# Handing Wo over from layer A to layer B: tiles cut to A's ending tiles, an earlier norm for B's second group, and a second bf16 row tile

## The chip, the cores and the metric

One core of a Trainium2 chip runs the whole kernel as one program. The metric is the device time of one execution in microseconds (us); the time of the kernel before is the median of 7 runs. The profile is one further execution with the hardware profiler on, whose span (first to last instruction) and own time are given below.

## The reference, cut to what matters

Activations x are [2048, 640]. Four layers follow one another, A, B, A, B, each adding its result to x after a layer norm without scale or offset:

```python
x = A_x
x = x + _A_ref(_layernorm(x), A_wq, A_wk, A_wv, A_wo, A_beta)
x = x + _B_ref(_layernorm(x), B_mem0, B_Wq, B_Wk, B_Wv, B_Wo, 32)
x = x + _A_ref(_layernorm(x), ...)      # same weights
x = x + _B_ref(_layernorm(x), ...)      # same weights
```

Layer A is causal attention of 32 heads of 20 in four blocks of 512 tokens, with a running memory `M`, `z` mixed in by a gate, and ends with `o @ wo`. Layer B is a recurrence over 64 segments of 32 tokens:

```python
for s in range(64):
    h = concat([mem, x[32*s:32*s+32]])          # 8 + 32 rows
    q, k, v = h @ Wq, h @ Wk, h @ Wv            # 32 heads of 128
    p = softmax(mask(q @ k.T * scale))
    o = einsum('bhte,hed->btd', p @ v, Wo)      # Wo: 32 heads x 128 x 640
    mem, out = o[:8], o[8:]                     # mem feeds the next segment
```

So every segment of B needs all 32 heads of `Wo` before it can hand its memory to the next one. `Wo` is 5.2 MB in bf16, and it is loaded anew for each of the two B layers.

## The kernel before, in words

**Order of the work.** All compute engines but SP (TensorE = PE, VectorE = DVE, ScalarE = ACT, GpSimd = POOL) run in the order in which the program writes the instructions: the wrapper `_OrdEng` ties each instruction to the one before it on its engine, which is why nearly all rows of the profile have its line, L87. The DMAs issued from SP are not tied in this way; a scheduler places them, and SP then issues them strictly one after another, each after its own waits. A DMA also waits for an earlier DMA on the same of eight completion lanes. Buffers come from pools; a tile may start to be written when the last reader of what lay there before is done.

**The end of layer A.** A's last eight half-row products, `outp(3, 0..7)` (tiles `a_YP`, one pair per row tile `tt` of 128 rows), are kept back as `br.tail` and are run among the first projections of B. Each pair adds the residual rows, giving the fp32 row tile (`a_xo` in the first handover, `a_xr` itself in the second), stores it to `xres` (L518), has POOL cast it to the bf16 tile `a_xb` (one buffer), and stores that to `xres_bf` (L521). The tiles of A that live until then are, on the right side of SBUF, `a_oT` (5120 bytes in each partition), `a_wvo` (6400) and `a_xb` (1280) in the pool `a_out`, and `a_xr`, `a_xo` in `a_out2`; and on the left side the pool `a_tail`, which `tail_tiles` fills with two residual rows and, in the first handover, an output row.

**Wo.** One head of `Wo` is 1280 bytes in each partition. Heads 0 to 10 (`EARLY`, `NEARLY` = 11) are loaded during the last block of A into tiles of A that are free by then (`a_wo`). Head 11 goes into a pool of its own (`b_wo1`), loaded from ACT's queue among B's first projections. Heads 12 to 15 (`b_wo3`, where `a_tail` was) and 16 to 31 (`b_wo2`, one tile of 16 heads in two loads, where A's `a_out` and `a_out2` were) are issued from SP once `a_tail` and `outer` are closed (L942 and L944). All of the second tile is taken to depend on all that lay under it.

**The start of layer B.** First come six tail units (`b_tail`: Q, K and V of the 32 last-rows of group 0; a group is 4 segments, 128 rows), then four first projections (`b_first`), each after one pair of A's tail. Then the loop over segments: `b_Qa`, `b_Ka`, `b_Qb`, `b_Kb` (projections; DVE turns each through one of two `b_TQ` buffers, DVE and POOL place it), `b_SP` (scores, three PSUM buffers shared with the projections), `b_V`, `b_OTL` (values) and `b_OPS`, the product with `Wo`: a first half with heads 0 to 15, and a second half in pairs (16,20) (17,21) (18,22) (19,23) (24,28) (25,29) (26,30) (27,31). The memory rows of `b_OPS` go through `b_TM` on DVE into `b_hT`, for which the next segment's `b_Qa` waits.

**The norm of group 1.** `ln_dma(1)` loads its rows at B's start. In segment 0 `ln_norm(1)` runs after the first values (two `BATCH_NORM_STATS2`, an aggregate, an add on DVE, a power on POOL), `ln_apply(1)` writes `b_xn` on DVE, and `ln_tr(1)` issues a transposing DMA to `b_xnTg` (L738), followed by the load of group 2's rows (L723). `tail_cols(1)` then copies columns of it to `b_hx` on POOL at the start of the tail units of segment 1; for later groups it runs in the segment before.

Of the kernel before, what the change touches and what calls it, by code (L numbers as in the profile page):

```python
# [19 lines left out]
BF16 = mybir.dt.bfloat16  # L20
# [3 lines left out]
PSUM = bass.MemoryType.PSUM  # L24

S_TOK = 2048
NW1 = 12
EARLY = [(tag, h0, n, at) for tag, h0, n in (("a_phiks", 0, 1), ("a_MZ32", 1, 2), ("a_xnT0", 3, 4), ("a_vaug0", 7, 4)) for at in range(n)]
NEARLY = len(EARLY)
ORDER_ENGINES = ("tensor", "scalar", "vector", "gpsimd")  # L30
D = 640
# [23 lines left out]
def layernorm_stats(nc, pool, C, xt, name):  # L55
    stats = pool.tile([128, 2, nc.vector.BN_STATS_DIM], F32, name=f"{name}_st", tag="ln_st")
    nc.vector.bn_stats(out=stats[:, 0, :], in_=xt[:, 0:320])
    nc.vector.bn_stats(out=stats[:, 1, :], in_=xt[:, 320:640])
    mv = pool.tile([128, nc.vector.BN_AGGR_DIM], F32, name=f"{name}_mv", tag="ln_mv")
    nc.vector.bn_aggr(out=mv[:], in_=stats[:])  # L60
    rstd = pool.tile([128, 1], F32, name=f"{name}_rstd", tag="ln_rstd")
    nc.vector.tensor_scalar(out=rstd[:], in0=mv[:, 1:2], scalar1=LN_EPS, scalar2=None, op0=ALU.add)
    nc.gpsimd.tensor_tensor(out=rstd[:], in0=rstd[:], in1=C.mhalf[:, 0:1], op=ALU.pow)
    return mv, rstd


def layernorm_apply(nc, xt, xn_out, mv, rstd):
    nc.vector.tensor_scalar(out=xn_out.rearrange("p (g jj d) -> p jj g d", jj=2, d=32),
                            in0=xt.rearrange("p (jj g d) -> p jj g d", jj=2, d=32),
                            scalar1=mv[:, 0:1], scalar2=rstd[:, 0:1], op0=ALU.subtract, op1=ALU.mult)  # L70
# [130 lines left out]
def layer_A(nc, nc_raw, tc, C, W, A_wv, A_wo, x_src, x_dst, xb_dst, src_is_bf16, general, outer, mem0, wo_src, prep=None, prefetch=()):  # L201
# [5 lines left out]
    with ExitStack() as ctx:  # L207
        br = Bridge()
        bp = outer.bridge.enter_context(tc.tile_pool(name="a_bridge", bufs=1, side="right", reuse_waits="tile"))
        so = outer.enter_context(tc.tile_pool(name="a_out", bufs=1, side="right", reuse_waits="tile"))  # L210
# [116 lines left out]
        def run(gctx):  # L327
# [13 lines left out]
            us, xin = {}, {}  # L341
# [158 lines left out]
            def res_load(n, tt):  # L500
                r0 = n * 512 + tt * 128
                xr = so2.tile([128, D], xdt, name="a_xr")
                nc_raw.sync.dma_start(xr[:], x_src[r0:r0 + 128, :])
                xin[tt] = xr

            def outp(n, i):
                tt, half = divmod(i, 2)
                if half == 0 and (tt, "o") not in xin:
                    xin[tt, "o"] = so2.tile([128, D], F32, name="a_xo") if src_is_bf16 else xin[tt]
                xo = xin.pop((tt, "o")) if half else xin[tt, "o"]  # L510
                hs = slice(320 * half, 320 * half + 320)
                YP = pg.tile([128, 320], F32, name="a_YP", tag="pg")
                for c in range(NCH):
                    nc.tensor.matmul(YP[:], lhsT=oT[:, c, 128 * tt:128 * tt + 128], rhs=wvo[:, c, hs], start=(c == 0), stop=(c == NCH - 1))
                nc.vector.tensor_tensor(out=xo[:, hs], in0=YP[:], in1=xin[tt][:, hs], op=ALU.add)
                if half:
                    r0 = n * 512 + tt * 128
                    nc_raw.sync.dma_start(x_dst[r0:r0 + 128, :], xo[:])  # L518
                    xb = so.tile([128, D], BF16, name="a_xb")
                    nc.gpsimd.tensor_copy(xb[:], xo[:])  # L520
                    nc_raw.sync.dma_start(xb_dst[r0:r0 + 128, :], xb[:])  # L521
                    if tt + 2 < 4 and n < NS - 1:
                        res_load(n, tt + 2)
# [117 lines left out]
            def tail_tiles(pool):  # L641

                for tt in (2, 3):
                    r0 = (NS - 1) * 512 + tt * 128
                    xin[tt] = pool.tile([128, D], xdt, name=f"a_xr{tt}")
                    nc_raw.sync.dma_start(xin[tt][:], x_src[r0:r0 + 128, :])
                if src_is_bf16:
                    xin[2, "o"] = pool.tile([128, D], F32, name="a_xo2")

# [29 lines left out]
def layer_B(nc, nc_raw, tc, C, W, br, outer, wo_src, x_src, xb_src, x_dst, general, nsteps=64, out_bf16=False):  # L679
# [3 lines left out]
    NT = nsteps // 4  # L683
    with ExitStack() as ctx:
# [2 lines left out]
        wk2 = ctx.enter_context(tc.tile_pool(name="b_wk2", bufs=2, reuse_waits="tile"))  # L687
        hp = qkp = sm = wk2
        wk = st
        wop = ctx.enter_context(tc.tile_pool(name="b_wo", bufs=1, reuse_waits="tile"))  # L690
        wo = [wop.tile([128, NW1 - NEARLY, D], BF16, name="b_wo1")]
        pp = ctx.enter_context(tc.tile_pool(name="b_ps", bufs=3, reuse_waits="tile", space=PSUM))

        tail_ctx = ExitStack()
# [2 lines left out]
        def wo_of(h):  # L697
            for t, h0, n in br.wo:
                if h0 <= h < h0 + n:
                    return t[:, h - h0]  # L700
            return wo[0][:, h - NEARLY] if h < NW1 else wo[1][:, h - NW1] if h < 16 else wo[2][:, h - 16]

        def ps_tile(shape, dtype, name):
            return pp.tile(shape, dtype, name=name, tag="ps")
# [21 lines left out]
        def ln_norm(g):  # L726
            xt = ln_x.pop(g)
            ln_n[g] = xt, layernorm_stats(nc, sm, C, xt[:], "b_ln")

        def ln_apply(g):  # L730
            xt, (mv, rstd) = ln_n[g]
            xn = ln_n[g] = be.tile([128, D], BF16, name="b_xn", tag="xn")
            layernorm_apply(nc, xt[:], xn[:], mv, rstd)

        def ln_tr(g):
            xn = ln_n.pop(g)
            xg = be.tile([128, NCH, 128], BF16, name="b_xnTg", tag=f"xnTg{g % 2}")
            nc.sync.dma_start(xg[:], xn[:], transpose=True)  # L738
            xnT_g[g] = xg
# [8 lines left out]
        def heads(t):  # L748
            return t[:].rearrange("p (h c) -> p h c", h=32)
# [30 lines left out]
        def thin_mm(ps, cols, Wt, b, wsel):  # L780
            for f in thin_parts(ps, cols, Wt, b, wsel):
                f()

        def turn(ps):

            tq = wk2.tile([128, 16, 32], F32, name="b_TQ", tag="TQ")
            nc.vector.transpose(out=tq[:].rearrange("p h t -> p (h t)"), in_=ps)
            return tq

        def place(eng, tq, b, dst3, t0, t1, c0):  # L790
            evac(eng, dst3[:, 16 * b:16 * b + 16, c0:c0 + (t1 - t0)], tq[:, :, t0:t1])
# [6 lines left out]
        def tail_cols(T):  # L798
            if T not in hx:
                hx[T] = wk.tile([128, NCH, 32], BF16, name="b_hx", tag="hx")  # L800
                v = xnT_g[T][:].rearrange("p c (i t) -> p c i t", t=32)[:, :, :, 24:32]
                nc.gpsimd.tensor_copy(hx[T][:].rearrange("p c (i t) -> p c i t", t=8), v)
            return lambda c: hx[T][:, c, :]
# [40 lines left out]
        def flush():  # L844
            while done:
                done.pop(0)()
# [66 lines left out]
        def tail(n=1):  # L913
            for _ in range(n):
                if rest:
                    rest.pop(0)()

        for kind in ("Q", "K", "V"):
            for b in range(2):
                TailUnit(0, kind, b).run(NCH)  # L920
                flush()
                h = NEARLY + {"K": 0, "V": 2}.get(kind, NW1) + b
                if h < NW1:
                    nc.scalar.dma_start(wo[0][:, h - NEARLY, :], wo_src[:, h, :])
        for Wt, dst in ((W.wq, QT), (W.wk, KT)):
            for b in range(2):
                h = NEARLY + 4 + (b if Wt is W.wq else NW1)
                if h < NW1:
                    nc.scalar.dma_start(wo[0][:, h - NEARLY, :], wo_src[:, h, :])
                tail(2)  # L930
                ps = ps_tile([128, 512], F32, "b_first")
                thin_mm(ps, lambda c: hT[0][:, c, 0:32], Wt, b, w_heads)
                place(("act", "pool")[b], turn(ps[:]), b, heads(dst[0]), 0, 24, 0)
# [3 lines left out]
        outer.close()  # L937
        wop3 = ctx.enter_context(tc.tile_pool(name="b_wo3", bufs=1, reuse_waits="tile"))
        wop2 = ctx.enter_context(tc.tile_pool(name="b_wo2", bufs=1, side="right", reuse_waits="tile"))
        wo.append(wop3.tile([128, 16 - NW1, D], BF16, name="b_wo3"))  # L940
        wo.append(wop2.tile([128, 16, D], BF16, name="b_wo2"))
        nc_raw.sync.dma_start(wo[1][:], wo_src[:, NW1:16, :])  # L942
        for a, b in ((16, 24), (24, 32)):
            nc_raw.sync.dma_start(wo[2][:, a - 16:b - 16, :], wo_src[:, a:b, :])  # L944
        po = ctx.enter_context(tc.tile_pool(name="b_po", bufs=1, reuse_waits="tile", space=PSUM))
        pot = ctx.enter_context(tc.tile_pool(name="b_pot", bufs=2, reuse_waits="tile", space=PSUM))

# [11 lines left out]
        for s in range(nsteps):  # L959
            last = (s == nsteps - 1)  # L960
            T, i4 = divmod(s, 4)
# [11 lines left out]
            elif T + 1 < NT:  # L973
                kind = " VQK"[i4]
# [173 lines left out]
            V1 = VPass(1)  # L1148
            V1.run(2)
            values(0)  # L1150
            g_need = (s + 6) // 4 if s % 4 == 2 else 1 if s == 0 else NT
            if g_need < NT:
                ln_norm(g_need)
            V1.run(3)
# [1 line left out]
            take("act", 0, 0)  # L1156
            take("act", 0, 1)
            normalise(1)
            if i4 == 0 and 1 <= T < NT - 1:
                tail_cols(T + 1)  # L1160
            if g_need < NT:
                ln_apply(g_need)
# [159 lines left out]
```

## Time and profile before

| what | value |
| --- | --- |
| median of 7 runs | 2266.2 us (2264.17 to 2269.62) |
| profiled execution: own time, span | 2267.44 us, 2265.7 us |
| mean granted TensorE clock | 0.982 |
| PE busy | 2151.7 us, 95% |
| DVE, POOL, ACT busy | 72%, 45%, 40% |
| layer A | about 0 to 286 us, and 1135 to 1407 us |
| first handover, second handover | about 286 to 338 us, 1407 to 1458 us |

Times in the profile are counted from the start of the span. A wait is listed with what ended it; a busy share near 100% of PE together with a clock below 1 means that PE is at work at half speed. In the segments of B away from the handovers PE has no gap but the one for `b_hT`.

### The profile page before, as it was taken

How to read it: one execution, taken by the hardware profiler on the slowest of the kernel's cores; microseconds unless marked ns; L12 is line 12 of the kernel's file. 1: busy time of each engine (PE TensorE's matmuls, PEld its weight loads, DVE VectorE, ACT ScalarE, POOL GpSimd, SP SyncE). 2: the span in 40 equal slices, each digit the busy share in tenths (PEclk: the TensorE clock that was granted, in tenths of full speed). 3: DMA queues.
4: the chain of work that ended last, by engine and by line, in shares of the span. 5: the costliest groups of instructions: out<-in, count | busy, mean ns of one | idle time of the engine just before them, and what ended most of it. 6: DMA issues, size and time to landing. Idle time of an engine off the chain costs nothing.

```text
span 2265.7 us, 122151 instructions
## 1 busy us (share of the span) xinstructions
PE 2151.7 (95%) x54486; PEld 1214.2 (54%) x54548; DVE 1634.7 (72%) x3998; ACT 909.7 (40%) x2111; POOL 1027.0 (45%) x2475
## 2 busy tenths in 40 slices
PE   6998889999999999999979999899999999999997
PEld 3444445555555555555544444455555565655554
DVE  5787647777776777777668887577777777777775
ACT  5776713333333233333357766223333333333332
POOL 3454434444454444444323545344444444444442
PEclk9999989999999999999989999999999999999999
DMA  6676840111110001010144665410101111010000
GB/s 165 165 177 170 225 127 22 23 27 22 24 21 24 22 22 26 23 25 15 28 111 123 151 161 141 120 24 20 20 19 20 20 21 20 19 24 19 18 13 14
DMA packets 150138, 137.79 MB, mean 61 GB/s; under 512 B 75984, under 2 KB 139488, under 8 KB 147680
## 3 DMA queue, kind: packets, MB, share of 16 engines
q1 hardware_dynamic: 147136, 126.60, 22.5%
q8 instruction: 428, 7.01, 1.3%
q10 hardware_dynamic: 2464, 3.28, 0.6%
q14 instruction: 110, 0.90, 0.1%
HBM read 89.17 MB, written 26.21 MB: 51 GB/s over the span
## 4 chain that ended last, share of the span: by engine, by line
PE 81%; DVE 7%; DMA 4%; ACT 3%; issue 2%; POOL 1%; SPq 1%; ACTq 0%; DVEq 0%; POOLq 0%
PE b_V L87 13%; PE b_OPS L87 12%; PE b_tail L87 10%; PE b_Qa L87 6%; PE b_Kb L87 6%; PE b_Ka L87 6%; PE b_Qb L87 6%; PE b_SP L87 5%; PE b_OTL L87 4%; PE a_PP L87 3%; PE b_OPSd L87 3%; ACT a_PT L87 2%; PE a_S L87 2%; PE a_pv L87 2%; PE a_VP L87 1%
## 5 line engine op out<-in xcount | busy, mean ns | idle before, releaser
L87 PEld LDWEIGHTS <-b_hT 128*32 128x32 bf16 x15120 | 378.1, 96 | 309.6 <-DVE b_hT L87 69.2
L87 ACT ACTIVATE b_PT<-b_SP 128x224 bf16<-128x224 f32 x256 | 92.3, 360 | 772.3 <-PE b_SP L87 738.8
L87 PE MATMUL b_V<-b_wv,b_hT 128*32 128x512 bf16 x5040 | 357.7, 381 | 0.0
L87 ACT ACTIVATE a_PT<-a_S 128x768 bf16<-128x768 f32 (+1 forms) x384 | 325.8, 884 | 75.2 <-PE a_S L87 58.7
L87 PE MATMUL b_OPS<-b_wo,b_OTsb 128*32 128x320 bf16 x5376 | 258.0, 301 | 11.9 <-DMA b_wo<-in_B_Wo_dram 7.4
L87 PEld LDWEIGHTS <-b_OTsb 128*32 128x32 bf16 x8192 | 200.9, 97 | 100.6 <-DVE b_OTsb L87 48.9
L87 POOL CAST b_QT<-b_TQ 128x384 bf16<-128x384 f32 x254 | 140.3, 552 | 227.4 <-DVE b_TQ L87 227.4
L87 ACT CAST b_OTsb<-b_OTL 128x320 bf16<-128x320 f32 x384 | 151.4, 428 | 202.9 <-PE b_OTL L87 183.7
L87 POOL CAST b_KT<-b_TQ 128x384 bf16<-128x384 f32 x254 | 142.8, 562 | 130.3 <-DVE b_TQ L87 126.9
L87 POOL TENSOR_TENSOR b_PT<-b_PT,b_R 128x64 bf16<-128x64 bf16 x256 | 105.4, 412 | 212.5 <-ACT b_R L87 197.2
L87 PE MATMUL b_Qa<-b_wq,b_hT 128*32 128x512 bf16 x2520 | 184.9, 386 | 5.0 <-DVE b_hT L87 5.0
L87 PE MATMUL b_Ka<-b_wk,b_hT 128*32 128x512 bf16 x2520 | 183.7, 384 | 0.0
L87 PE MATMUL b_Kb<-b_wk,b_hT 128*32 128x512 bf16 x2520 | 183.0, 380 | 0.0
L87 POOL TENSOR_SCALAR_AFFINE_SELECT a_PT<-a_PT 128x256 bf16<-128x256 bf16 x256 | 109.4, 431 | 160.9 <-ACT a_PT L87 158.5
L87 DVE STREAM_TRANSPOSE b_TM<-b_OPS 128x128 f32<-128x128 f32 x252 | 88.3, 350 | 127.1 <-PE b_OPS L87 123.2
L87 PE MATMUL b_Qb<-b_wq,b_hT 128*32 128x512 bf16 x2520 | 158.4, 379 | 0.0
L87 PE MATMUL a_PP<-a_xnT,a_wt 128*128 128x512 bf16 x505 | 140.9, 392 | 15.4 <-ACT a_phiq L87 4.8
L87 PE MATMUL a_S<-a_qk 32*128 32x512 bf16 (+3 forms) x1024 | 137.0, 308 | 7.7 <-ACT a_PT L87 6.4
L87 DVE CAST b_Vsb<-b_V 128x512 bf16<-128x512 f32 x128 | 88.6, 692 | 77.0 <-PE b_SP L87 49.5
L87 PE MATMUL b_OPS<-a_wo,b_OTsb 128*32 128x320 bf16 x2816 | 143.6, 299 | 0.0
L87 DVE CAST b_OTsb<-b_OTL 128x320 bf16<-128x320 f32 x128 | 63.0, 492 | 96.7 <-PE b_OTL L87 96.7
L87 POOL TENSOR_TENSOR b_Rtot<-b_Rtot,b_R 128x160 bf16<-128x160 bf16 x256 | 127.1, 497 | 0.0
(158 smaller groups left out, 4277.8 us busy)
## 6 DMA issues: line engine op xcount, KB each, us to landing
a_wt<-a_wpad SPq DMA_DIRECT2D x112, 160.0 KB
b_XO<-xres SPq DMA_DIRECT2D x256, 30.0 KB
a_wvo<-in_A_wo_dram SPq DMA_DIRECT2D x8, 800.0 KB
b_wq<-in_B_Wq_dram SPq DMA_DIRECT2D x20, 256.0 KB
b_wk<-in_B_Wk_dram SPq DMA_DIRECT2D x20, 256.0 KB
xres<-a_xo SPq DMA_DIRECT2D x16, 320.0 KB
xres_bf<-a_xb SPq DMA_DIRECT2D x32, 160.0 KB
b_wv<-in_B_Wv_dram SPq DMA_DIRECT2D x20, 256.0 KB
```

Of the source, the lines that this page charges most:

```text
L87: r = f(*a, **k)
```

## The change

It has three parts.

1. `Wo` after the early heads: `b_wo1` and the two loads of `b_wo2` go. There are four tiles, each with one load from SP: heads 25 to 30, 11 to 19 and 31 on the right side (7680, 11520 and 1280 bytes in each partition, in this order) and heads 20 to 24 on the left (6400 bytes). They are loaded in the order 11 to 19, 20 to 24, 25 to 30, 31.
2. `ln_norm(1)`, `ln_apply(1)` and `ln_tr(1)` move from segment 0 to between the tail units and the first projections. `tail_cols(1)` moves into segment 0, as in the other groups.
3. A second bf16 row tile `a_xb1` in the pool `a_tail`; the row tiles `tt` = 1 and 3 of A's tail use it in place of `a_xb`.

```diff
-NW1 = 12
@@ layer_A, outp
-                    xb = so.tile([128, D], BF16, name="a_xb")
+                    xb = xin.get("b") if tt % 2 else None
+                    xb = xb if xb is not None else so.tile([128, D], BF16, name="a_xb")
                     nc.gpsimd.tensor_copy(xb[:], xo[:])
                     nc_raw.sync.dma_start(xb_dst[r0:r0 + 128, :], xb[:])
@@ layer_A, tail_tiles
                     nc_raw.sync.dma_start(xin[tt][:], x_src[r0:r0 + 128, :])
+                xin["b"] = pool.tile([128, D], BF16, name="a_xb1")
                 if src_is_bf16:
                     xin[2, "o"] = pool.tile([128, D], F32, name="a_xo2")
@@ layer_B
-        wop = ctx.enter_context(tc.tile_pool(name="b_wo", bufs=1, reuse_waits="tile"))
-        wo = [wop.tile([128, NW1 - NEARLY, D], BF16, name="b_wo1")]
+        wo = []
@@ layer_B, wo_of
-            return wo[0][:, h - NEARLY] if h < NW1 else wo[1][:, h - NW1] if h < 16 else wo[2][:, h - 16]
+            return next(t[:, h - a] for t, a, b in wo if a <= h < b)
@@ layer_B, tail units and first projections
                 TailUnit(0, kind, b).run(NCH)
                 flush()
-                h = NEARLY + {"K": 0, "V": 2}.get(kind, NW1) + b
-                if h < NW1:
-                    nc.scalar.dma_start(wo[0][:, h - NEARLY, :], wo_src[:, h, :])
+        ln_norm(1)
+        ln_apply(1)
+        ln_tr(1)
         for Wt, dst in ((W.wq, QT), (W.wk, KT)):
             for b in range(2):
-                h = NEARLY + 4 + (b if Wt is W.wq else NW1)
-                if h < NW1:
-                    nc.scalar.dma_start(wo[0][:, h - NEARLY, :], wo_src[:, h, :])
                 tail(2)
@@ layer_B, after A's tail
-        wo.append(wop3.tile([128, 16 - NW1, D], BF16, name="b_wo3"))
-        wo.append(wop2.tile([128, 16, D], BF16, name="b_wo2"))
-        nc_raw.sync.dma_start(wo[1][:], wo_src[:, NW1:16, :])
-        for a, b in ((16, 24), (24, 32)):
-            nc_raw.sync.dma_start(wo[2][:, a - 16:b - 16, :], wo_src[:, a:b, :])
+        parts = [(wop2, 25, 31), (wop2, NEARLY, 20), (wop2, 31, 32), (wop3, 20, 25)]
+        parts = [(pool.tile([128, b - a, D], BF16, name=f"b_wo_{a}"), a, b) for pool, a, b in parts]
+        for i in (1, 3, 0, 2):
+            wo.append(parts[i])
+            t, a, b = parts[i]
+            nc_raw.sync.dma_start(t[:], wo_src[:, a:b, :])
@@ layer_B, segment loop
-            g_need = (s + 6) // 4 if s % 4 == 2 else 1 if s == 0 else NT
+            g_need = (s + 6) // 4 if s % 4 == 2 else NT
...
-            if i4 == 0 and 1 <= T < NT - 1:
+            if i4 == 0 and T < NT - 1:
                 tail_cols(T + 1)
```

The order of the instructions on PE is the same in both kernels. On DVE the group 1 norm now stands between the last turn of the tail units and A's first residual add; on POOL its power stands before the first cast to `a_xb`. On SP the transpose to `b_xnTg` and the load of `b_xt` stand after the second of the `b_XOd` loads, ahead of the stores of A's first tail rows, and the four `Wo` loads stand together after the last store to `xres_bf`.

## The prediction

> **What bounds the kernel now.** I read the page first, then the waits of PE, then the two handovers by window, by chain and by row.
>
> From the page, the chain that ended last:
>
> ```profile
> PE 81%; DVE 7%; DMA 4%; ACT 3%; issue 2%; POOL 1%; SPq 1%; ACTq 0%; DVEq 0%; POOLq 0%
> ```
>
> PE carries four fifths of it, so what PE does not wait for or does not run at half clock comes off the end. The waits of PE, first window 285 to 330 us, then 1130 to 1470 (total, times, longest, us):
>
> ```profile
> PE b_OPS L87 <- DMA b_wo<-in_B_Wo_dram: 4.9, 2, 4.1
> PE b_SP L87 <- DVE b_TQ L87: 2.5, 1, 2.5
> PE b_SP L87 <- DVE b_KT L87: 0.4, 1, 0.4
> PE b_OTL L87 <- issue: 0.3, 1, 0.3
> ...
> PE b_OPS L87 <- DMA b_wo<-in_B_Wo_dram: 2.5, 1, 2.5
> PE b_OTL L87 <- issue: 2.5, 1, 2.5
> PE b_SP L87 <- DVE b_TQ L87: 2.2, 1, 2.2
> PE b_tail L87 <- POOL b_hx L87: 1.3, 1, 1.3
> ```
>
> The windows (PE, PEld, DVE, ACT, POOL busy us; granted clock; DMA share; GB/s) show what follows a long wait:
>
> ```profile
> 315.00:320.00 5.00, 3.57 (x132) 2.37 (x121) 2.59 (x7) 2.00 (x6) 3.07 (x9) 1.00 1.05 366
> 320.00:325.00 5.00, 1.11 (x16) 0.50 (x15) 0.00 (x0) 0.00 (x0) 0.00 (x0) 0.86 1.03 209
> 325.00:330.00 5.00, 4.17 (x44) 1.54 (x44) 2.16 (x8) 0.00 (x0) 0.00 (x1) 0.50 0.01 3
> 1435.00:1440.00 5.00, 2.56 (x97) 1.73 (x97) 1.81 (x6) 1.40 (x4) 1.24 (x3) 1.00 1.05 358
> 1445.00:1450.00 5.00, 4.17 (x47) 1.47 (x44) 2.06 (x7) 0.00 (x0) 0.00 (x0) 0.50 0.01 3
> ```
>
> While `Wo` comes in at some 365 GB/s, PE starves; then 5 us at clock 0.50. The chain of the first handover (start, us, what) says why `Wo` is late:
>
> ```profile
> 300.85 2.82 DMA xres_bf<-a_xb
> ...
> 304.57 1.80 DMA xres_bf<-a_xb
> ...
> 306.52 0.73 POOL a_xb L87
> ...
> 307.27 1.80 DMA xres_bf<-a_xb
> ...
> 309.88 0.52 POOL b_KT L87
> ...
> 310.43 0.73 DVE b_TQ L87
> ...
> 313.50 10.35 DMA b_wo<-in_B_Wo_dram
> ```
>
> One `a_xb` buffer makes cast, store and landing alternate, some 2.7 us a row. Behind the last cast POOL owes `b_KT`, DVE owes the turn of Ka, PE owes `b_SP`; and heads 16 to 31 start only when the last row has landed.
>
> **The change, part by part.** Each figure is for the first / second handover, on the profiled execution.
>
> *Second row tile.* Row 1 is cast at once (its add ends at 299.05). With the transpose (1.23 us of SP at 318.06) and the `b_xt` load (0.57) now ahead, less two `b_XOd` issues (0.34 each), row 0's store moves from 300.85 to about 301.9 and lands near 304.5. The transpose itself waits for `b_xn`, written near 295.6, and SP comes by at 298.6: no wait. Row 2 is cast to 305.3; row 1's store, at 304.2, lands at 306.0; row 3 is cast to 306.9, against 309.94. `b_KT` then ends near 307.4, and Ka's turn runs after Qa's, 307.65 to 308.4. PE reaches `b_SP` at 308.7, so the waits of 2.49 and 2.20 go: -4.7. If row 0 lands 1 us later than this, 0.6 comes back; bounds -3.5 and -4.9. The 0.43 for `b_KT` I leave in both.
>
> *Norm among the first projections.* DVE does 2 x 0.435 + 0.21 + 0.15 + 0.44 = 1.67 us, and stands meanwhile for POOL's power (0.55 and 0.24 to reach it), 293.1 to 295.65. Queued behind it is A's first residual add, which ran at 295.23: 0.4 late. DVE had 0.79 us idle before the next turn and PE needs that PSUM buffer at 296.99, so nothing reaches PE: 0; without that cover, 0.4 each. Taking the same work out of segment 0 gives 0 too, DVE having been idle there.
>
> *`b_hx` a segment earlier.* The copy (0.31 on POOL) moves to a place where PE is busy; PE's 1.3 goes in both: -2.6 (elsewhere this kind of segment shows no such wait). At worst POOL's later copies slip 0.3 each.
>
> *`Wo` in four loads.* 21 heads of 164 KB are 3.44 MB, at 365 GB/s 9.4 us. The first load has only PE's last read of `a_oT`, `a_wvo` to wait for and is issued after row 3's store, near 307.5 (before: heads 16 to 31 at 313.06). Data flow from 308.3; heads 11 to 19 are in by 313, 20 to 24 by 315, 25 to 30 by 318.0, 31 by 318.3. SP waits 1.8 us for row 3 to land before the second load; the 4.0 us of the first cover that. With the fetch stall of the next part, `b_OPS` needs head 28 near 318.8. So 4.10 + 0.2 and 2.52 go: -6.8; bounds -4.2 (1.3 left in each, if PE gets there sooner) and -6.8.
>
> *Instruction fetch.* The trace's records of the instruction queue show PE being fed in 16384-byte packets, one for some 250 recorded PE instructions. In the second handover the packet that PE stood for (2.49 us in `b_OTL`) started at 1434.56, 2.9 us after PE passed the previous boundary, took 1.28 us, and PE went on 1.52 us later. In the first it started 0.8 us after, before the big loads, and PE lost 0.31. With `Wo` earlier, both such fetches meet a full DMA: +2.2 / 0. The next packet took 3.8 and 3.6 us to start; PE will reach that boundary some 6 us on, about 0.5 short: +1.0 in all. Sum +3.2; bounds -2.8 (no stall) and +6.
>
> The Trainium skill ("Runtime: NRT & Kernel Launch", section Instruction fetch mechanics) holds that fetches are hidden by the sequencer's own pace and cost next to nothing at a block boundary. By it this term would be -2.8 and the total 6.0 us better; the 2.49 us row speaks against it, and the sum goes by the row.
>
> *Clock.* The trace has the clock at half from 323.64 to 330.47 and 1443.21 to 1450.04. In these PE ran 0.73 us of `b_OPS` in 1.26, and worked 4.5 and 3.9 us at half: (0.53 + 2.25) + (0.53 + 1.96) = 5.3 us lost. Each follows a stretch of 3.41 us in which PE worked 0 and 1.07 us; one with 1.9 us of work (1432.97 to 1436.39) did not cost it. With the long `Wo` wait gone the remaining gap is about 2.5 us, which mostly falls across two stretches: -5.3. Where it falls into one, some 0.9 us of work is left in it and the clock drops again; by (3.41 - 2.5) / 3.41 that is 3 in 10 in each handover, 2.65 us each.
>
> The Trainium skill ("TensorE: Matmul & The Clock Gate", Part 1) asks for a whole idle window before the clock falls; by it 2.5 us could never do it. The second handover, with 1.07 us of work in the window, fell all the same, so I keep the 3 in 10.
>
> *SP and ACT.* ACT's queue loses one issue (0.36), where it was idle: 0.
>
> Sum: -4.7 - 2.6 - 6.8 + 3.2 - 5.3 = -16.2. The profiled execution's 2267.44 becomes 2251.2; it stands 1.2 above the median, so 2250.0 for the median.
>
> **The rivals.**
>
> *The clock drops again* in one or both: -16.2 + 2.65 or 5.3, 2252.7 to 2255.3. For: the second drop came with a third of the stretch in work. Against: only 3 in 10 places of the gap do it.
>
> *The fetch is quicker than I take it*, since the loads are spread and the transpose is out of them: no stall, but up to 1.3 us of `Wo` wait back in each: -16.2 - 6.0 + 2.6 = -19.6, 2246.6. For: 0.31 in the first handover. Against: 2.49 in the second, with the DMA just as full.
>
> *The wait changes its name*: row 0's store, behind transpose and `b_xt`, lands so late that the casts are spaced as before. Then -4.7 is lost, `Wo` starts 2 us later and keeps 2 us of wait in each, and the clock falls: -16.2 + 4.7 + 4 + 5.3 = -2.2, 2264.0. For: nine small DMAs and a transpose stand close together there. Against: the transpose's input is written 3 us before SP comes to it.
>
> *Slower*: SP stands at the transpose until it has landed, and with it the stores of all four rows and all `Wo` loads. A like one of A took 4.90 us from issue to landing (270.50, `a_bxnT`). The `b_XOd` load on its lane does wait for it, but from 298.6 that ends at 303.5, when row 1's store would come anyway. To cancel 16.2 us the hold must be over 8.1 us longer in each handover, that is past 311.6; at 11 it gives +5.8, 2272. Against: no transpose in the trace holds SP for over 2.6 us.
>
> **How the numbers follow.** Forecast 0.55, clock again 0.24, quicker fetch 0.11, wait renamed 0.06, slower 0.04. Within 0.2% (4.5 us, about what a measurement can tell from no change) lies most of the renamed wait; so faster 0.90, same 0.06, slower 0.04. The range takes in the quick fetch with the full `b_SP` gain, and at the other end both clock drops with the 2.6 of `Wo` wait and the 1.2 of `b_SP` back (2259.1): 2245 to 2260.
>
> **What would show it.** In the profile after: the `b_SP` waits for `b_TQ` under 0.5; no `b_OPS` wait for `b_wo` over 1.3; no `b_tail` wait for `b_hx`; the first big load at about 307.5 and 1427.3; an `issue` wait of `b_OTL` near 2.5 in both handovers; clock 1.00 after them. Wrong would be: a clock of 0.50 after either, SP idle before the first `xres` store of A's tail, or a `b_OTL` wait gone.

## The result, and the profile after

| what | before | after |
| --- | --- | --- |
| median on the first chip | 2266.99 us (33 runs) | 2256.72 us (13 runs, 2249.26 to 2264.26) |
| ratio, 95% interval | | 0.9952 [0.994, 0.9964], about -10.9 us |
| median on a second chip | 2272.54 us (17 runs) | 2262.98 us (12 runs) |
| ratio, 95% interval | | 0.9962 [0.9948, 0.9975], about -8.6 us |
| profiled execution: own time, span, clock | 2267.44, 2265.7, 0.982 | 2261.81, 2259.7, 0.978 |
| second profile of the changed kernel | | 2258.82, 2256.7, 0.984 |

The kernel is faster, by about two thirds of what was forecast on the first chip and about half on the second, where the second profile was taken too. Every wait that the prediction meant to remove is gone, and the clock gain that it counted on did not come. The line of the page for the chain that ended last is nearly as it was:

```profile
PE 82%; DVE 7%; DMA 3%; ACT 3%; issue 2%; SPq 1%; POOL 1%; ACTq 0%; DVEq 0%; POOLq 0%
```

The waits of PE in the same two windows as before, the rows on B's tiles (total, times, longest, us; the second window starts at the first "...", and the next ones stand for rows on A's tiles):

```profile
PE b_OTL L86 <- issue: 3.2, 1, 3.2
PE b_Qa L86 <- DVE b_hT L86: 0.8, 1, 0.8
PE b_OPS L86 <- DVE b_OTsb L86: 0.6, 1, 0.6
PE b_SP L86 <- DVE b_KT L86: 0.4, 1, 0.4
...
PE b_OTL L86 <- issue: 3.7, 1, 3.7
...
PE b_OPS L86 <- DVE b_OTsb L86: 1.3, 2, 0.7
...
PE b_Qa L86 <- DVE b_hT L86: 0.8, 1, 0.8
```

`b_SP` no longer waits for `b_TQ`, `b_OPS` no longer for `b_wo`, and no unit waits for `b_hx`. In their place stands one long wait in each handover that is listed as `issue`: the profile shows no other engine and no load that PE waited for. SP's timeline in the first handover (start, us, instructions) shows the rows leaving and the loads following at once:

```profile
306.14 1.15 SPq L521 DMA_DIRECT2D xres_bf<-a_xb  x1
...
308.90 0.36 SPq L521 DMA_DIRECT2D xres_bf<-a_xb  x1
...
309.85 0.41 SPq L521 DMA_DIRECT2D xres_bf<-a_xb  x1
...
312.15 0.32 SPq L521 DMA_DIRECT2D xres_bf<-a_xb  x1
312.56 4.80 SPq L942 DMA_DIRECT2D b_wo<-in_B_Wo_dram  x4
```

A ended 4.9 us later in this execution, so times are compared from the first `b_first` product (295.80 before, 300.67 after): the first large load was expected at 11.7 and came at 11.9. The windows of the second handover, cut at the steps of the clock (PE, PEld, DVE, ACT, POOL busy us; granted clock; DMA share; GB/s), show what was not expected:

```profile
1428.62:1432.03 3.41, 1.45 (x71) 0.75 (x63) 0.77 (x3) 1.27 (x4) 1.35 (x3) 1.00 1.06 374
1432.03:1435.45 3.42, 1.69 (x37) 0.86 (x41) 0.00 (x0) 0.75 (x2) 0.00 (x0) 0.50 1.07 359
1435.45:1438.86 3.41, 2.79 (x76) 1.52 (x72) 1.51 (x3) 1.07 (x3) 1.72 (x6) 0.50 0.45 151
1438.86:1442.27 3.41, 2.58 (x36) 1.13 (x35) 1.04 (x4) 0.00 (x0) 0.80 (x3) 0.50 0.02 5
1442.27:1445.69 3.42, 3.42 (x36) 1.26 (x32) 0.86 (x3) 0.00 (x0) 0.00 (x0) 0.50 0.00 0
```

The stall falls across the first two stretches, and from the second on the clock is at half for four stretches, 13.65 us. The first handover is the same (319.29 to 332.94). Before, half clock lasted 6.83 us in each.

### The profile page after: what moved, and what is told of

Read it like the earlier page. It is cut to its first block, busy times and chain, and to the rows that moved or that the text cites. A ratio compares the mean times of both kernels' runs of the same rounds, so it can differ in the third digit from the quotient of the medians.

```text
span 2259.7 us, 122155 instructions
## 1 busy us (share of the span) xinstructions
PE 2156.7 (95%) x54486; PEld 1209.9 (54%) x54548; DVE 1632.5 (72%) x3998; ACT 909.6 (40%) x2111; POOL 1027.9 (45%) x2475
## 4 chain that ended last, share of the span: by engine, by line
PE 82%; DVE 7%; DMA 3%; ACT 3%; issue 2%; SPq 1%; POOL 1%; ACTq 0%; DVEq 0%; POOLq 0%
PE b_V L86 13%; PE b_OPS L86 13%; PE b_tail L86 10%; PE b_Qa L86 6%; PE b_Kb L86 6%; PE b_Ka L86 6%; PE b_Qb L86 6%; PE b_SP L86 5%; PE b_OTL L86 4%; PE a_PP L86 3%; PE b_OPSd L86 3%; ACT a_PT L86 2%; PE a_S L86 2%; PE a_pv L86 2%; PE a_VP L86 1%
## 5 line engine op out<-in xcount | busy, mean ns | idle before, releaser
L86 PEld LDWEIGHTS <-b_hT 128*32 128x32 bf16 x15120 | 373.1, 96 | 313.4 <-DVE b_hT L86 69.7
```

The lines of the kernel that those rows point to most:

```text
L86: r = f(*a, **k)
```

## The experiments

All ratios are to the kernel before, run on the same chip. Two questions were open: what the `b_OTL` stall is, and what each part of the change is worth. Theory P: PE has run to the end of a fetched block of instructions, and the packet with the next one stands in the DMA behind the `Wo` loads. Rival O: the stall has its cause elsewhere, at those instructions or in that place of the order, and the packet only happens to be there. To see when a packet was due, count back 256 recorded PE instructions (one more for each extra wait) from the stalled product; that place is called its boundary here.

**The stall.**

*One head per load* (same bytes, 21 loads instead of 4):

```diff
-            nc_raw.sync.dma_start(t[:], wo_src[:, a:b, :])
+            for h in range(a, b, 1):
+                e = min(h + 1, b)
+                nc_raw.sync.dma_start(t[:, h - a:e - a, :], wo_src[:, h:e, :])
```

> The late Wo loads of the changed kernel, one head (164 KB) per DMA: 21 loads in place of 4. Theory P (a fetch packet has to stand behind what the big loads have queued in one go on a DMA engine, and the clock falls because of that wait): the fetch of the block that PE waits for starts within 1.5 us of the boundary, the issue wait of b_OTL in the first segment of B is under 1.0 in both handovers, the clock stays at 1.00 there, and the time is 2240 to 2248. Rival S (any full DMA holds the fetch back, however the loads are cut): the issue wait stays at 3 to 4 us, the clock falls, the time stays at 2254 to 2260.

2258.71 us, 0.9962 [0.9948, 0.9977]. Waits of PE in the two handovers:

```profile
PE b_OPS L86 <- DMA b_wo<-in_B_Wo_dram: 2.4, 3, 2.0
...
PE b_OTL L86 <- issue: 0.3, 1, 0.3
...
PE b_OPS L86 <- DMA b_wo<-in_B_Wo_dram: 2.0, 2, 1.6
...
PE b_OTL L86 <- issue: 0.9, 1, 0.9
```

The packets started 1.3 and 1.6 us after their boundaries, against 4.1 and 4.3 in the changed kernel, and the stall shrank from 3.2 and 3.7 to 0.3 and 0.9: P. The time did not follow: it lies where rival S had it. Neither did the clock: it was at half for 6.8 and 10.2 us, where 1.00 had been expected. SP issued the 21 loads without a pause in 11.8 and 11.3 us, about 0.55 us each, the stream fell from some 360 to 380 GB/s to about 280, and `b_OPS`, now reached sooner, waited for it. What the stall had covered came out under its own name.

*No late loads* (leaves out the `Wo` loads of heads 11 to 31, whose products use early heads instead):

```diff
-            return next(t[:, h - a] for t, a, b in wo if a <= h < b)
+            return wo_of(h % NEARLY)
@@
-            nc_raw.sync.dma_start(t[:], wo_src[:, a:b, :])
```

> Leaves out the loads of heads 11 to 31 of Wo; these heads are multiplied with the early tiles in their place, with the same instructions on PE. Theories P and S (the loads cause the wait for instructions): no issue wait of b_OTL over 0.5 in the first segment, clock 1.00 through both handovers, 2238 to 2246. Rival I (PE runs through these blocks faster than any fetch can follow, whatever the DMA does): the wait of 3 us stays.

2244.27 us, 0.9898 [0.9878, 0.9919]. The stall fell to 0.4 in the second handover but stayed at 1.9 in the first, and the clock still fell, to half for 10.2 and 3.4 us. In the first handover the DMA was not empty: with `Wo` left out, SP issued the 800 KB load of `a_wvo` for the next A layer at 308.26, and the DMA moved 314 GB/s from 310.2 to 312.6, just before the packet started at 312.58. The changed kernel issues no such load there, and behind the second handover there is no A. So another large load stood before that packet; that it made the 1.9 us was not tested by itself. This is the only kernel clearly beyond the changed one: some 12 us still lie in the loads and in what they cause.

*All block boundaries moved by 128 instructions* (64 small products at the start of the program):

```diff
+        if prep:
+            wm = pg.tile([128, 512], F32, name="a_shift", tag="pg")
+            for _ in range(64):
+                nc.tensor.matmul(wm[0:32, 0:32], lhsT=C.identb[:, 0:32],
+                                 rhs=C.identb[:, 0:32], start=True, stop=True)
```

> 64 small matmuls (128 PE instructions) stand at the program's start, where PE waits for its first input; their result is not used. All later block boundaries of 256 instructions move 128 instructions forward in the program. Theories P and S: the issue wait of some 3 us leaves the end of the first b_OTL group and stands about 128 instructions after or before it (b_V, b_SP or the second b_OTL group); time within 4 us of the changed kernel's 2256.7, either way. Rival O (the wait belongs to b_OTL, to its PSUM tile or the evacuated V, and is only called issue): it stays at the end of the first b_OTL group.

2258.31 us, 0.997 [0.9957, 0.9984]. The first group of `b_OTL`, which had stalled in both handovers, had no stall. It came later, 2.0 us in the second `b_OTL` group of the first handover and 1.6 in `b_OPS` of the second (waits of PE, first and second handover):

```profile
PE b_OTL L86 <- issue: 2.0, 1, 2.0
...
PE b_OPS L86 <- issue: 1.6, 1, 1.6
```

Counted from the first `b_first` product, the stalled instruction is the 658th and the 635th recorded one of PE in the two handovers of the kernel before and of the changed one, in both its profiles; here it is the 787th and the 762nd, 129 and 127 further on. It moves with the boundary: O falls. Some of the other waits came back with the shorter stall: 1.6 and 1.3 us of `b_SP` for `b_TQ`, 0.9 and 2.2 of `b_OPS` for `b_wo`. A last count supports P in all profiles: in all 26 `issue` waits of over 0.25 us in the handovers of the 14 profiles, PE went on 1.2 to 1.6 us after the records show the packet moved.

**The parts.**

*Only the second row tile.*

```diff
-                    xb = so.tile([128, D], BF16, name="a_xb")
+                    xb = xin.get("b") if tt % 2 else None
+                    xb = xb if xb is not None else so.tile([128, D], BF16, name="a_xb")
@@
+                xin["b"] = pool.tile([128, D], BF16, name="a_xb1")
```

> The kernel before with the second bf16 row tile alone. By the prediction's sum: the b_SP waits for b_TQ of 2.5 and 2.2 go, Wo starts some 2.5 us sooner, and of the Wo waits about as much stays as before less what the earlier start gives, since segment 0 starts sooner too: -4.7 for the b_SP waits, 2261 to 2263. Rival (the fetch meets the loads sooner and gives it back): 2265 to 2268, with an issue wait of b_OTL over 2 us in both handovers.

2257.89 us, 0.9967 [0.9951, 0.9983], about -7.5 us. Waits of PE, first and second handover:

```profile
PE b_OTL L87 <- issue: 3.6, 1, 3.6
...
PE b_OTL L87 <- issue: 4.2, 1, 4.2
```

The `b_SP` waits for `b_TQ` are gone, and so is the `Wo` wait but for 0.4 us, although the tiles are the old ones: the loads start when the rows are out, and the longer stall hides their end. The stall is the one that the rival of the expectation named, but its time, 2265 or more, did not come; the sum's 2261 to 2263 was too slow as well.

*Only the norm* (with the old tiles and one row buffer):

```diff
+        ln_norm(1)
+        ln_apply(1)
+        ln_tr(1)
@@
-            g_need = (s + 6) // 4 if s % 4 == 2 else 1 if s == 0 else NT
+            g_need = (s + 6) // 4 if s % 4 == 2 else NT
@@
-            if i4 == 0 and 1 <= T < NT - 1:
+            if i4 == 0 and T < NT - 1:
```

> The kernel before with the norm of group 1 moved, and tail_cols(1) with it, alone. By the prediction's sum: the two b_hx waits of 1.3 go, and the transpose on SP now stands ahead of the stores of A's rows, which with one a_xb costs up to 1 us at the b_SP wait: 2264 to 2267 (ratio 0.9985 to 1.0). Rival (the transpose ahead holds the stores for its 4.9 us): b_SP waits of 4 to 5 us, 2270 or more.

2267.18 us, 1.0 [0.9989, 1.0011]. Waits of PE, first and second handover:

```profile
PE b_SP L87 <- DVE b_TQ L87: 2.8, 1, 2.8
PE b_OPS L87 <- DMA b_wo<-in_B_Wo_dram: 2.7, 1, 2.7
...
PE b_SP L87 <- DVE b_TQ L87: 3.8, 1, 3.8
PE b_OPS L87 <- DMA b_wo<-in_B_Wo_dram: 3.4, 1, 3.4
```

`b_hx` is gone, but with the transpose ahead of the stores `b_SP` waits 0.3 and 1.6 us longer (2.5 and 2.2 before), and the clock was at half for 13.66 us in each handover. So 1.9 of the 2.6 us goes there, and the time shows no gain.

*Only the tiles* (the changed kernel with one row buffer and the norm in its old place).

```diff
-                    xb = xin.get("b") if tt % 2 else None
-                    xb = xb if xb is not None else so.tile([128, D], BF16, name="a_xb")
+                    xb = so.tile([128, D], BF16, name="a_xb")
@@
-        ln_norm(1)
-        ln_apply(1)
-        ln_tr(1)
...
```

> The kernel before with the four Wo tiles alone. One a_xb as before, so the b_SP waits of 2.5 and 2.2 stay; the first load of nine heads can start at about the time of the old one of four, so the Wo waits of 4.1 and 2.5 fall under 1. Theory P (the instruction fetch then waits for the loads, and the clock falls): issue waits of b_OTL of 2 to 4 us in both, clock at half for 7 to 14 us, 2263 to 2268, no clear gain. Rival (the tiles are what the change's gain comes from): 2256 to 2261.

2260.43 us, 0.9975 [0.9961, 0.999], about -5.7 us. No `Wo` wait, `b_SP` still waits 2.6 and 2.7 us, `b_hx` 1.1 and 1.3, and the stall is 3.1 and 4.2, as P expected, but the time is the rival's. The profile is of one of its longest executions (2269.42 us, where the 12 runs go from 2255.62 to 2270.84).

*Row tile and norm, old tiles* (the edits of the first two together).

> The second row tile and the moved norm, without the new Wo tiles. After e4 (2257.9 with the row tile alone): if the norm's 2.6 us at b_hx come through, 2254 to 2257, and the new tiles bring nothing to the change; if the new tiles bring their share, this stays at 2258 to 2261, above the changed kernel.

2258.01 us, 0.9965 [0.9952, 0.9978]. The stall is 2.5 and 1.8, and the `Wo` waits are back at 2.2 and 4.2. The shorter stall covers less of them. The time is that of the row tile alone.

*Row tile and tiles, the norm in its old place.*

> The changed kernel without the moved norm: second row tile and Wo tiles. If the norm's part is worth its 2.6 us (b_hx waits of 1.3 come back in both), 2258 to 2261; if it is worth nothing, as e5 has it (2267.2 against 2266.9), 2255 to 2258, no different from the changed kernel; if its transpose costs at the stores, 2252 to 2255.

2258.2 us, 0.9975 [0.9963, 0.9987]. Stall 3.1 and 3.3; `b_hx` keeps its 1.3 in both.

The parts alone give -7.5, 0 and -5.7, together -13.2; all at once gave -10.9 and -8.6. The intervals (some 3 us to each side) tell neither the pairs, nor the row tile alone, nor the sum of the parts from the whole; what the norm and the tiles add to the row tile is not shown in the times. If the whole is less than the sum, the waits offer a reason: the row tile alone already removes most of the `Wo` wait.

**Trying to keep the short stall and the fast stream.**

*Two heads per load.*

```diff
-            nc_raw.sync.dma_start(t[:], wo_src[:, a:b, :])
+            for h in range(a, b, 2):
+                e = min(h + 2, b)
+                nc_raw.sync.dma_start(t[:, h - a:e - a, :], wo_src[:, h:e, :])
```

> The changed kernel with two heads (328 KB) per Wo load. One head per load had the fetch 0.7 us after the boundary, but moved Wo at some 280 GB/s in place of 365, since SP needs about 0.58 us per load. Theory P2 (the handover is bound by two things, the fetch behind large loads and the end of the Wo stream, and each hides the other): fetch within 1.5 us, stream near 360 GB/s, ending some 23 us after the start of b_first; a b_OPS wait for b_wo of 1 to 2.5 us takes the place of the issue wait; 2252 to 2257. Rival (only the fetch counts): no wait over 1 us, clock 1.00, 2242 to 2248.

2258.87 us, 0.9963 [0.9949, 0.9976]: stall 2.2 and 2.1, `Wo` waits 0.5 and 2.0. Packets started 2.8 and 2.6 us after their boundaries. The kernel stands between the four loads and the twenty-one, in both waits; the time is 2 us slower than was expected at most.

*The same, with heads 11 to 19 from ACT's queue.*

```diff
-                nc_raw.sync.dma_start(t[:, h - a:e - a, :], wo_src[:, h:e, :])
+                (nc.scalar if i == 1 else nc_raw.sync).dma_start(t[:, h - a:e - a, :], wo_src[:, h:e, :])
```

> As e8 (two heads per load), with heads 11 to 19 issued from ACT's queue, which is free from 8 us after the start of b_first, in place of SP's, where they stand behind A's last stores until 12 us. Theory P2 (fetch behind large loads, and the end of the Wo stream, bind together): the stream starts some 3 us earlier and ends near 20 us after the start of b_first, no b_OTL issue wait over 2.5 and no b_OPS wait for b_wo over 1; 2246 to 2254. Rival C (whatever wait is taken away, the granted clock falls somewhere in the handover and takes the gain): 2256 to 2260.

2255.15 us, 0.9963 [0.995, 0.9976]. In the first handover ACT stood at its loads, and `b_SP` waited 6.4 us for ACT's `b_PT`; the second had a 3.0 us stall and no half clock at all. There the packet started 3.7 us late, though the loads had two heads each. Loss and luck in one profile, and a ratio like the others.

*The four loads, the first from ACT's queue* (the same edit on the single load).

> The changed kernel with its load of heads 11 to 19 on ACT's queue, the loads as large as they were. Theory P: the stream ends sooner, but the fetch stands behind 1.5 MB loads as before: issue wait of b_OTL 3 to 5 us, clock down, 2255 to 2260, above e9 by some 4. Rival (only the end of the stream counts): as e9, 2246 to 2254.

2257.26 us, 0.9969 [0.9955, 0.9983]: stall 0.9 and 2.8, `Wo` waits 2.9 and 1.3. Packets started 1.9 and 3.4 us after their boundaries. The time is as P expected, but a stall of 3 to 5 us was expected with it: a short stall came here with loads as large as before, so the size of the loads does not set it alone.

No version beats the changed kernel. All variants that keep the loads and change the rows or the loads lie between 0.995 and 0.998.

**The changed kernel once more**, unaltered.

> The changed kernel, unaltered, for a second profile and a second interval. Theory (the waits of the prediction are gone for good, the clock falls as the execution has it): the same rows of waits at the handovers as in the first profile, b_OTL's issue stall between 2.5 and 4 us in both, no wait of b_SP for b_TQ, none of b_OPS for b_wo, none of b_tail for b_hx; but the stretches at half clock differ from the first profile's 13.65 us per handover, anything from 0 to 13.65 us, and the profiled span moves with them by some 0.4 us for each us at half clock; time 2252 to 2261 us, ratio 0.994 to 0.997. Rival (the changed order of work makes the clock fall this way, each time): 13.65 us at half clock at both handovers again.

2262.98 us, 0.9962 [0.9948, 0.9975] on the second chip. The stall is there again, 3.1 and 3.3 us; 0.4 of `b_TQ` came back in the first handover and 0.6 of `b_wo` in the second. But half clock lasted 3.41 us in the first handover, and there was none in the second. Windows of the second handover of this profile, columns as above:

```profile
1421.63:1425.04 3.41, 1.83 (x79) 0.98 (x71) 1.15 (x3) 1.58 (x5) 1.35 (x3) 1.00 1.04 363
1425.04:1428.46 3.42, 1.67 (x57) 1.18 (x61) 0.60 (x1) 1.20 (x4) 0.00 (x0) 1.00 1.07 359
1428.46:1431.87 3.41, 2.09 (x74) 1.21 (x70) 0.91 (x3) 0.62 (x2) 2.44 (x8) 1.00 0.55 185
```

Here the stretches cut the stall nearly in half, 1.83 and 1.67 us of work are left, and the clock stays. In the first profile 1.45 us were left and it fell. Much the same waits, then, with 27.3 us at half clock in one execution and 3.4 in another; the rival expectation, that the new order makes the clock fall this way each time, is wrong.

## Why the prediction was right and wrong

2256.72 us lies in the range, 6.7 us above the point. By its terms:

**Second row tile, right.** -4.7 was forecast for the `b_SP` waits, and they are gone (0.4 in one handover of the second profile). `b_KT`'s 0.43 stayed in the first handover, as said, and is 0.14 in the second.

**Norm, right in the sum, with a condition not stated.** 0 on DVE holds, and -2.6 for `b_hx` holds as a wait in the whole change; in the times it is not shown (2258.2 us without the norm). The experiment with the norm alone shows that it needs the second row buffer: without it, with the transpose ahead of the stores, 1.9 of the 2.6 comes back at `b_SP`.

**`Wo`, right, under the cover named.** The `Wo` waits went, -6.8. The text let the fetch stall cover the last heads and gave 1.3 us per handover as the price without it. With one head per load that cover was taken away, and 2.4 and 2.0 came back, on a stream that was slower too.

**Fetch, right in kind, off in size.** 2.5 us per handover was taken and 3.2 and 3.7 measured. The second boundary, priced at 1.0, cost nothing in either profile. The term was +3.2 and measured (3.2 + 3.7) - 2.8 = +4.1. The Trainium skill ("Runtime: NRT & Kernel Launch", Instruction fetch mechanics) describes blocks of 256 instructions, which the shift by 128 agrees with, and holds their fetch to be mostly hidden. Behind the large loads 3.1 to 3.7 us in four handovers do not bear that out. Away from the handovers it is nearly so: of the 8.5 us that PE of the kernel before waited in `b_OTL` on `issue`, in 18 waits, 5.7 lie there, in pieces of at most 0.7. (The description of the kernel before says that PE has no gap there but the one for `b_hT`; these pieces are gaps too.)

**Clock, the step that failed.** It gave -5.3 for a clock that would no longer fall, and 3 in 10 per handover that it would. By its own figures that is a chance of 0.51 for at least one fall, where the list of rivals has 0.24, and the sum took the -5.3 whole. In the first profile the clock fell in both handovers and stayed down twice as long as before, which the prediction had named as a sign of being wrong. The price of this comes from the two profiles of the changed kernel. In the second handover the `b_Qa` of segment 2 comes 42.72 us after the first `b_first` in one and 39.12 in the other. Of these 3.60 us, 0.4 is a longer stall and -0.6 the missing `b_wo` wait, so 13.65 us at half clock cost 3.8. The first handover gives 3.4 for 10.24 us likewise. That is some 0.3 us for each us, less than half; PE is not busy all the while (21.4 of the 27.3 us at half clock in the first profile). So the first profile lost 27.3 x 0.3 = 8.2. At the same price the 13.66 us before had cost 4.1, and not the 5.3 that the prediction worked out.

With that the two profiles nearly close. From first `b_first` to the `b_Qa` of segment 2, both handovers together took 92.76 us before. By the terms measured the first profile should save 4.7 + 2.6 + 6.8 - 4.1 - (8.2 - 4.1) = 5.9, and the records give 92.76 - 85.40 = 7.4. The second should save 4.3 + 2.6 + 6.2 - 3.6 + (4.1 - 1.0) = 12.6, and the records give 14.05. The 1.5 us left over in each is open; that it is the same in both is no second proof, since the price was taken from the difference of the two. Of the first profile's 7.4, 5.6 reached its own time: A's first pass ended 4.9 us later, with 34.1 us at half clock in it against 27.3 before, and most but not all of that came back later. The second profile is from the other chip, so its 14.05 can be set only roughly against a profile of the first.

For the median, the mean granted clock tells more than a profile. Over the 12 and 17 executions of the last comparison it was 0.981 for the changed kernel and 0.981 for the one before. Over the whole kernel, then, the clock gained nothing on average; what it did in the handovers alone is known for the profiles only. -16.2 without its -5.3 is -10.9, and the two chips measured -10.9 and -8.6. That the first agrees to a tenth is luck: the fetch term is 0.9 off, the -5.3 more likely 4.1, and the intervals are some 3 us to each side. The spread of the changed kernel's times is the clock too: over 15 executions on the first chip, the profiled one among them, time falls by 1.4 us for each 0.001 of mean clock (correlation -0.87). Over some 2260 us, 0.001 of mean clock is 4.5 us at half clock, so this gives 0.3 us for each too. The rival that the prediction called "the clock drops again" is what took place in the first profile. It had a chance of 0.24 and a price of 2.65 per handover, and cost 8.2 / 2 = 4.1 there.

**Why the chance was wrong.** The prediction read off two falls and one stay that about 0.9 us of work in a stretch decides. With 14 profiles at hand the mark can be read better. Take the stretches that begin within 42 us after the first `b_first` product of each handover. Of 289 at full clock, all 24 in which PE was busy for at most 46% were followed by half clock, 3 of 7 from 47 to 50%, and 2 of 258 above that (at 55% and 69%). So here a stretch falls with about 1.7 us idle in it. A gap of 2.5 us, wherever it lies in stretches of 3.41, puts that much into one of them (1.7 + 0.8) / 3.41, about 7 times in 10, and one of 3.4 us nearly always, unless it is cut in half as above, where 49% was left in one stretch and the clock could have gone either way. The second slip is the length. Of 65 stretches at half clock, none of the 29 below 80% busy was followed by full clock, 3 of 10 from 80 to 82%, and all 26 above. The stall lies in `b_OTL`; behind it come values and `b_OPS` with their own small waits, 49 to 82% busy at half clock, and only the projections of the next segment fill a stretch. Before, the fall came one stretch ahead of those. A fall earlier in the segment lasts longer.

These counts come from kernels made for other questions; no run set the share on purpose. And the mark does not hold elsewhere: at the end of A, with other products, the clock fell after stretches in which PE was busy for 2.82 of 3.41 us (to 1402.25, before) and 2.92 (to 1397.90, after). So the busy share is not what the clock goes by; what is, these runs do not show. The Trainium skill ("TensorE: Matmul & The Clock Gate", Part 1) has the fall follow a whole idle window of 3.4 us. The window's length agrees; falls after stretches at 45% and 42% busy in the first profile contradict the rest. The prediction had set that rule aside for its row with 1.07 us of work, and still took the mark too low.

**The slower rival**, SP held at the transpose, did not come: the four rows of the first handover left within 0.7 us of the forecast, and the first load came 0.2 us off its time.

## What to carry to other kernels

Write down the waits and the clock as two accounts: a gap is paid once as a wait, and again as half clock if (in these handovers) it leaves less than about half of some 3.41 us stretch in work, so trimming a gap from 4 us to 3 saves 1 us and will mostly keep the fall. Before counting a wait as gone, ask what stands beside it: here the end of the `Wo` stream and the instruction fetch hid each other, and each edit that shortened one brought out the other. Where executions of one kernel differ by 15 us, look at the mean clock of each before explaining a single profile.

## What the hardware showed that was not expected

- The clock falls after a partly busy stretch: in these handovers at or below 46% in 24 of 24 cases, against 2 of 258 above 50%; at the end of A after stretches at 83% and 86% too. In the handovers it comes back only after a stretch that is at least 80% busy at half clock (29 of 29 returns). At half speed 80% of a stretch is 40% of its full work, so in the handovers one mark on the work done in a stretch could explain both; that was not tested.
- An instruction packet that is due while large loads are moving starts late: 1.3 and 1.6 us after its boundary with one head (164 KB) per load, 2.8 and 2.6 with two heads, 3.8 to 4.3 with the four loads of the changed kernel in four handovers. The size of the loads is not all: with the first load on ACT's queue it was 3.7 us with two heads, and 1.9 and 3.4 with the large loads.
- Loads of 164 KB from one queue reached about 280 GB/s, with SP issuing one every 0.55 us without a pause; larger ones reached some 360 to 380. That SP's issuing is the limit was not tested.
